# An attention and feed-forward kernel: the weight blocks of TensorE moved to 144 and 192 bytes past the moving rows

## The chip, the cores and the metric

One core of a Trainium2 chip runs the whole program. The metric is device time in microseconds (us), the median of three runs. TensorE (PE in the profile) multiplies, VectorE (DVE), ScalarE (ACT) and GpSimd (POOL) do the rest, and SyncE (SP) issues most of the DMAs.

## The reference

```
q, k, v: (4, 8, 768, 64)   x = attention output, reshaped to (3072, 512)
keep   = (key < n_sink) or (0 <= query - key < window)      n_sink 4, window 128
a      = softmax(where(keep, q k^T / 8, -1e9));  x = a v
h      = x @ w_in            (512 -> 2048)
out    = (h - tanh(h)) @ w_out   (2048 -> 512)
```

All values are float32.

## The kernel before

The 3072 tokens are cut into twelve chunks of 256 (`chunks`), the 2048 inner features into eight groups of 256 (`NG`). A step is one pair (chunk, group); there are 96 of them in the list `order`. The first three chunks (cc below 3) run early with weights that lie in SBUF; the other nine stream their first weights from DRAM through a ring of seven slots (`stream`, L784).

A float32 operand is split into a high and a low part of type float32r, and a product is the sum of high by high, high by low and low by high. So a step needs in `mm1` (L794 to 807) 2 x 4 x 3 = 24 products of 128x128 weights with 256 moving columns of x, and 24 x 96 = 2304 in all. The second half of a step comes in two kinds. In 41 steps it is `mm2` (L869 to 877): 12 products with 512 moving columns each, 492 in all. In the other 55 it is `mm7` (L907 to 911), a scheme of seven half-size products: 21 products of 256 columns, 1155 in all. The scores of the later chunks (L524) are 288 products of 260 columns.

For TensorE a product is two instructions. The weight load brings the *stationary* block, 128 values (512 bytes) of each partition, into the array; the multiplication then passes the *moving* rows through it, 256 columns being 1024 bytes of each partition. In `mm1` the weights are stationary and x moves; in `mm2` and `mm7` the gated activations (`ghbuf`, `glbuf`) are stationary and the weights of the second matrix move.

Tiles come from pools, and a pool's place in SBUF follows from the order in which the pools are opened and from the sizes of the tiles. This sets the byte at which each operand starts on its partition. In the program before, modulo 256: the weight tiles of `wpool` start at 0; the ring in `rpool` at 64, since `wtile` (L317) leaves out `FAR` = 80 elements; its second half `spare`, `ghbuf` and `glbuf` at 64; the x parts of `xall` at 0 for the later chunks and at 64 for chunks 0 and 1 (`x_high`, L678 to 686); the x parts of chunk 2 at 64 (high, `bpool`) and 0 (low, `hpool`). Since the blocks follow each other in steps of 512 bytes, the distance from the moving rows to the stationary block, modulo 256, is the same for all products of a kind:

| products | moving at | stationary at | distance | count |
|---|---|---|---|---|
| L807, chunks 3 to 11 | 0 | 64 | 64 | 1728 |
| L911 | 0 | 64 | 64 | 1155 |
| L807, chunks 0 to 2 | 64 or 0 | 0 or 64 | 192 (448), 0 (120), 64 (8) | 576 |
| L877 (512 columns) | 0 | 64 | 64 | 492 |
| L524 (260 columns) | 0, 16, 128, 144 | 64 | 64, 48, 192, 176 | 288 |
| L666 (512 columns) | 0 | 192 | 192 | 24 |

The order of the instructions on each engine is found at build time by a planner (`Work.order`) from costs and due times that are numbers in the code. It knows nothing of addresses.

Of the kernel before, what the change touches and what calls it, by code (L numbers as in the profile page):

```python
# [18 lines left out]
P = 128  # L19
# [20 lines left out]
@with_exitstack  # L40
def kernel(
    ctx: ExitStack,
    tc: tile.TileContext,
    qd: bass.AP,
    kp: bass.AP,
    vp: bass.AP,
    vs: bass.AP,
    nsw: bass.AP,
    w_in: bass.AP,
    w_out: bass.AP,  # L50
    xd: bass.AP,
    out: bass.AP,
):
    nc = tc.nc

    cpool = ctx.enter_context(tc.tile_pool(name="cpool", bufs=1))
    ident = cpool.tile([P, P], F32, tag="ident", name="ident")
    nswi = cpool.tile([P, 32], I32, tag="nswi", name="nswi")[:, :4]

    pts = cpool.tile([P, NPAIR, 2, 4, P], F32, tag="pt", name="pt")  # L60
    early = []
    for m in range(2):
        first = pts[:, m].rearrange("p h a b -> p (h a b)")
        early.append((first[:, :KW], first[:, KW : KW + 2 * CH].rearrange("p (h s) -> p h s", h=2)))
    et = mybir.EngineType
    with tc.manual_schedule(engines={et.PE, et.SP, et.DVE, et.Activation, et.Pool}):

        scr = pts[:, 2, 0]
        nc.sync.dma_start(nswi, nsw.partition_broadcast(P))
        for m in range(2):  # L70
            k, q = early[m]
            nc.sync.dma_start(k, kp[0, m, :, :KW])
            _load_pair(nc, q, qd[0, 2 * m : 2 * m + 2, :, :CH], True)
            if m == 0:
                make_identity(nc, ident)
                nc.gpsimd.iota(scr[:, 0, :].bitcast(I32), pattern=[[-1, P]], base=0, channel_multiplier=1)
                nc.gpsimd.iota(scr[:, 1, :].bitcast(I32), pattern=[[1, P]], base=0, channel_multiplier=0)
        masks = _masks(nc, cpool, nswi, scr)
        _, (nlo, nhi, wlo, whi) = nc.values_load_multi_w_load_instructions(
            nsw[0:1, 0:4], skip_runtime_bounds_check_because="every value takes one of the two branches"  # L80
        )
        bad = nhi | whi | ((nlo + 3) >> 3) | ((wlo - 1) >> 7)


        WARM = 3
        with tc.tile_pool(name="warm", bufs=1, space=PSUM) as wp:
            warm = wp.tile([P, P], F32, tag="warm", name="warm")
            for _ in range(WARM):
                nc.tensor.matmul(warm, lhsT=ident, rhs=ident, start=True, stop=True)

    with tc.If(bad == 0) as cmp:
        _banded(tc, qd, kp, vp, vs, masks, w_in, w_out, ident, pts, early, out)
    with cmp.Else():
        _general(tc, qd, kp, vp, nswi, w_in, w_out, ident, xd, out)

# [8 lines left out]
        nc.sync.dma_start(q[r, h, :], src[h, r])  # L104


def _masks(nc, pool, nswi, scr):

    mask = pool.tile([P, 3, TS], F32, tag="mask", name="mask")
    above = pool.tile([P, P], F32, tag="above", name="above")
    below = pool.tile([P, P], F32, tag="below", name="below")
    after = pool.tile([P, P], F32, tag="after", name="after")
    lim = pool.tile([P, 2], F32, tag="lim", name="lim")
    diff, col, tmp = (scr[:, i, :] for i in range(3))
    nc.gpsimd.memset(mask[:, 0, :NSK], NEG)
    nc.vector.tensor_copy(diff, diff.bitcast(I32))
    nc.vector.tensor_copy(col, col.bitcast(I32))  # L120
    nc.vector.tensor_scalar(above, diff, 0.0, None, op0=ALU.is_lt)
    nc.vector.tensor_scalar(below, diff, 0.0, None, op0=ALU.is_le)
    nc.vector.tensor_scalar(after, diff, 0.0, None, op0=ALU.is_gt)
    nc.vector.scalar_tensor_tensor(diff, above, float(P), diff, op0=ALU.mult, op1=ALU.add)
    nc.vector.tensor_scalar(tmp, above, NEG, None, op0=ALU.mult)
    nc.vector.tensor_copy(lim[:, 0:1], nswi[:, 0:1])
    nc.vector.tensor_copy(lim[:, 1:2], nswi[:, 2:3])
    n_sink, window = lim[:, 0:1], lim[:, 1:2]
    nc.vector.tensor_scalar(mask[:, 2, NSK:], diff, window, NEG, op0=ALU.is_ge, op1=ALU.mult)
    nc.vector.tensor_scalar(col, col, n_sink, NEG, op0=ALU.is_ge, op1=ALU.mult)  # L130
    nc.vector.tensor_tensor(mask[:, 0, NSK:], mask[:, 2, NSK:], tmp, op=ALU.min)
    nc.vector.tensor_tensor(mask[:, 0, NSK:], mask[:, 0, NSK:], col, op=ALU.max)

    near, edge, sink = diff[:, :NSK], tmp[:, :NSK], col[:, :NSK]
    nc.vector.tensor_scalar(near, near, window, None, op0=ALU.is_lt)
    nc.vector.tensor_tensor(edge, edge, near, op=ALU.mult)
    nc.vector.tensor_tensor(mask[:, 1, :NSK], edge, sink, op=ALU.min)

    def rest():
        nc.scalar.copy(mask[:, 1, NSK:], mask[:, 2, NSK:])  # L140
        nc.scalar.copy(mask[:, 2, :NSK], sink)

    return mask, above, below, after, rest
# [86 lines left out]
        return sorted(start, key=lambda n: (start[n], n)), start  # L230


def _banded(tc, qd, kp, vp, vs, masks, w_in, w_out, ident, pts, early, out):
    nc = tc.nc
    et = mybir.EngineType
    with ExitStack() as ctx:

        def pool(name, bufs, **kw):
            return ctx.enter_context(tc.tile_pool(name=name, bufs=bufs, **kw))

        cpool, wpool, rpool, gpool = (pool(n, 1) for n in ("cpool", "wpool", "rpool", "gpool"))
        vpool = pool("vpool", 3)
        bpool, wmpool, qpool, kpool, hpool, xpool = (
            pool(n, 1) for n in ("bpool", "wmpool", "qpool", "kpool", "hpool", "xpool")
        )
        pp, sm = pool("pp", 2), pool("sm", 4)
        xall = xpool.tile([P, 4 * NPAIR * CH + 16], F32R, tag="xall", name="xall")
        ps, ps_h = pool("ps", 1, space=PSUM), pool("ps_h", 2, space=PSUM)
        dpool = pool("dpool", 1, space=bass.MemoryType.DRAM)

        banks = {n: ps.tile([P, 512], F32, tag=n, name=n) for n in ("s0", "s1", "o0", "o1", "t", "x")}
# [3 lines left out]
        wide = wmpool.tile([P, 2, 4, TS], F32, tag="wide", name="wide")  # L255
        flat = wide.rearrange("p a b c -> p (a b c)")
        gbuf = gpool.tile([P, 8, P], F32, tag="gbuf", name="gbuf")
        ghbuf = gpool.tile([P, 2, 7, P], F32R, tag="ghbuf", name="ghbuf")
        glbuf = gpool.tile([P, 8, P], F32R, tag="glbuf", name="glbuf")
        wscr = dpool.tile([NG, P, 2 * WG], F32, tag="wscr", name="wscr")  # L260
        bscr = dpool.tile([NG, P, 5, DM // 2], F32, tag="bscr", name="bscr")
        kscr = dpool.tile([2, P, 2, DM // 2], F32, tag="kscr", name="kscr")
# [33 lines left out]
        def home(cc):  # L296

            return cc if cc < 3 else cc % 2

        def raw(u):  # L300
            return u < RAW

# [9 lines left out]
        lent = {u: ((1, 7), (1, 5), (1, 6), (0, 6))[(u - 4) // 2] for u in range(4, RAW)}  # L312
        place_of = {}

        FAR = 80

        def wtile(k, g, dtype, name):  # L317
            if k == 0 and g % NSLOT == 1:
# [10 lines left out]
        def load_qk(u):  # L329
            cc, p, b, c = unit(u)  # L330

            def lend():
                if u == 3:
                    if u not in place_of:
                        place_of[u] = gpool.tile([P, 3 * WG // 2], F32, tag="spare", name="qk3")
                    return place_of[u]
                if lent[u] not in place_of:
                    k, g = lent[u]
                    place_of[lent[u]] = wpool.tile([P, 2 * WG], F32, tag=wtag(k, g), name=f"qk{u}")
                return place_of[lent[u]][:, u % 2 * WG : u % 2 * WG + WG]  # L340
# [72 lines left out]

        sides = cpool.tile([P, 4], F32, tag="sides", name="sides")
        sidei = cpool.tile([P, 16], I32, tag="sidei", name="sidei")[:, :4]
        half, odd = sides[:, 0:2], sides[:, 2:4]
        vsink = cpool.tile([P, 2, P], F32R, tag="vsink", name="vsink")
        vraw = cpool.tile([P, P], F32, tag="vraw", name="vraw")  # L420
# [53 lines left out]
        def split(u):  # L474
# [2 lines left out]

            def k_high(h):
                if h == 0:
                    t = hpool.tile([P, NPAIR * CH], F32R, tag="ha", name=f"ks{u}")  # L480
                    ks[u] = t[:, : 2 * (KW + 24)].rearrange("p (h k) -> p h k", h=2)[:, :, :KW]
                r = slice(64 * h, 64 * h + 64)
                nc.scalar.copy(ks[u][r, h, :], kt[u][r, :])  # L483
# [23 lines left out]
        def scores(u, t):  # L507
# [21 lines left out]
            def merge():  # L529
                ps = sps[u, t]  # L530
                if t == 0:
                    if slot(u) > 1:
                        pr[u] = wide[:, slot(u) - 2]
                    else:
                        pr[u] = pp.tile([P, 4, TS], F32, tag="p", name=f"p{u}")
                    st[u] = sm.tile([P, 12], F32, tag="st", name=f"st{u}")
                for h in range(2):
                    if kind > 0:
                        nc.vector.copy_predicated(ps[h][:, TS:WIN], above.bitcast(U32), ps[h][:, :P])
# [102 lines left out]
        def attend(cc, p0, pairs):  # L642
# [35 lines left out]
            def x_high(i):  # L678
                if p0 == 0 and i == 0:
                    if home(cc) == 2:  # L680
                        xh[cc] = bpool.tile([P, NPAIR, CH], F32R, tag="hb", name=f"xh{cc}")
                        xl[cc] = hpool.tile([P, NPAIR, CH], F32R, tag="ha", name=f"xl{cc}")
                    else:
                        at = 2 * NPAIR * CH * (1 - home(cc)) + 16 * (cc < 3)
                        both = xall[:, at : at + 2 * NPAIR * CH].rearrange("p (k n c) -> p k n c", k=2, n=NPAIR)
                        xh[cc], xl[cc] = both[:, 0], both[:, 1]
                r = slice(p0 + 2 * i, p0 + 2 * i + 2)
# [96 lines left out]
        def stream(n, j):  # L784
# [2 lines left out]
            if "a" not in ring:  # L787
                ring["a"] = wtile(0, 1, F32R, "ring").rearrange("p (i c) -> p i c", i=4)
            if i > 3 and "b" not in ring:
                ring["b"] = gpool.tile([P, 3, WG // 2], F32R, tag="spare", name="spare")  # L790
            ring[i] = ring["b"][:, i - 4, :] if i > 3 else ring["a"][:, i, :]
            nc.sync.dma_start(ring[i].bitcast(F32), wscr[g][:, j * WG // 2 : (j + 1) * WG // 2])

# [20 lines left out]

        def halves(n):
            r = n % 2
            return ghbuf[:, r].rearrange("p b t -> p (b t)")[:, : 2 * CH], glbuf.rearrange("p b t -> p (b t)")[:, r * 2 * CH : (r + 1) * 2 * CH]

        def gate(n):
            g0 = gbuf.rearrange("p b t -> p (b t)")[:, : 2 * CH]  # L820
# [542 lines left out]
```

## Time and profile before

| | us |
|---|---|
| median of three runs | 678.68 |
| the three runs | 681.78, 678.13, 678.68 |
| span of the profiled execution | 676.2 |

The profiled execution's span, from its first instruction to its last, is 676.2 us; what lies around it in a timed run is the remaining 2.5 us of the median. PE is TensorE's multiplication, PEld its weight load, which runs beside the multiplication before it. The chain view follows the work back from the last instruction, each time to what released it; a row such as "2.72 PE h L807 x24" is 24 products that start one behind the other in 2.72 us, so 113 ns apart. This distance from start to start is the price of a product here; the duration of one (about 280 ns) is the time through the pipeline.

### The profile page before, as it was taken

The numbers are of one execution on the slowest core, as the hardware profiler recorded it, in microseconds if no ns is written. First come the engines' busy times: TensorE is split into PE (matmuls) and PEld (weight loads), VectorE is DVE, ScalarE is ACT, GpSimd is POOL, SyncE is SP. The second block draws the span as 40 slices with busy tenths as digits, with TensorE's granted clock in tenths as the row PEclk, the third lists the DMA queues.
The fourth block names the chain that finished last, engine by engine and source line by source line (L and its number), as shares of the span: only waits on it lengthen the run. The fifth ranks groups of instructions, "written<-read, shape, count | busy, mean of one in ns | idle before, by whom it ended". The sixth has DMA issues, their size and how long they took to land.

```text
span 676.2 us, 14570 instructions
## 1 busy us (share of the span) xinstructions
PE 655.5 (97%) x5099; PEld 603.3 (89%) x5099; DVE 531.8 (79%) x1365; ACT 412.6 (61%) x1056; POOL 204.0 (30%) x363
## 2 busy tenths in 40 slices
PE   6899999999999999999999999999999999999995
PEld 4677899998988899889999999999999999999995
DVE  6889998964898975567798898888988878855654
ACT  4986443435998876556776667567667567632331
POOL 5454000001995443344523323332223322300100
PEclk9999999999999999999999999999999999999998
DMA  5878797786998677799977767867777766657861
GB/s 177 266 262 269 266 295 263 270 287 175 191 203 274 203 217 223 227 280 266 300 217 240 224 199 207 260 196 203 227 231 216 242 199 199 198 165 207 270 198 37
DMA packets 79341, 152.96 MB, mean 226 GB/s; under 512 B 9564, under 2 KB 25564, under 8 KB 79260
## 3 DMA queue, kind: packets, MB, share of 16 engines
q1 hardware_dynamic: 65884, 121.65, 57.4%
q0 software_dynamic: 13376, 30.30, 16.4%
q8 instruction: 42, 0.69, 0.4%
q14 instruction: 39, 0.32, 0.1%
HBM read 131.47 MB, written 20.45 MB: 225 GB/s over the span
## 4 chain that ended last, share of the span: by engine, by line
PE 73%; ACT 7%; DVE 5%; DMA 5%; POOL 4%; issue 4%; POOLq 0%; SPq 0%; DVEq 0%; ACTq 0%
PE h L807 30%; PE s L911 10%; PE o L911 7%; PE o L877 6%; PE x L672 3%; PE s L877 3%; DMA w<-bscr 2%; PE t L609 2%; PE t L672 2%; PE t L877 2%; PE t L524 2%; PE x L877 2%; ACT p L575 2%; PE x L524 1%; ACT p L549 1%
## 5 line engine op out<-in xcount | busy, mean ns | idle before, releaser
L807 PE MATMUL h<-xall,ring 128*128 128x256 f32 x990 | 130.9, 279 | 0.0
L807 PEld LDWEIGHTS h<-xall,ring 128*128 128x128 f32 x990 | 121.2, 188 | 0.9 <-PE t L672 0.2
L826 ACT ACTIVATE gbuf<-h 128x512 f32<-128x512 f32 x96 | 57.1, 595 | 84.6 <-PE h L807 55.2
L356 POOL DMA_DIRECT2D qraw<-qd x36 | 29.3, 813 | 222.4 <-DVE q L496 198.0
L807 PE MATMUL h<-xall,spare 128*128 128x256 f32 x738 | 96.2, 277 | 0.0
L807 PEld LDWEIGHTS h<-xall,spare 128*128 128x128 f32 x738 | 90.0, 188 | 0.5
L549 ACT ACTIVATE p<-p,st 128x132 f32<-128x132 f32 x168 | 66.9, 400 | 26.8 <-DVE st L541 25.5
L845 ACT CAST ghbuf<-gbuf 128x896 fp32r<-128x896 f32 x55 | 51.9, 943 | 49.3 <-DVE gbuf L842 48.8
L848 DVE TENSOR_TENSOR glbuf<-gbuf,ghbuf 128x896 fp32r<-128x896 f32 x55 | 60.3, 1096 | 19.7 <-ACT ghbuf L845 16.0
L575 ACT ACTIVATE p<-p,st 128x132 f32<-128x132 f32 x168 | 54.2, 394 | 3.9 <-DVE st L570 3.5
L829 DVE TENSOR_TENSOR gbuf<-h,gbuf 128x512 f32<-128x512 f32 x55 | 37.8, 687 | 19.1 <-ACT gbuf L826 18.7
L877 PE MATMUL o<-w,ghbuf 128*128 128x512 f32 x192 | 50.8, 399 | 0.3
L629 POOL TENSOR_TENSOR pt<-pt,after 128x512 f32<-128x512 f32 x32 | 44.4, 1386 | 22.0 <-ACT pt L626 21.3
L807 PE MATMUL h<-xall,w 128*128 128x256 f32 x384 | 50.5, 282 | 0.0
L807 PEld LDWEIGHTS h<-xall,w 128*128 128x128 f32 x384 | 48.5, 188 | 1.6
L829 DVE TENSOR_TENSOR h<-h,gbuf 128x512 f32<-128x512 f32 x41 | 28.5, 694 | 19.1 <-ACT gbuf L826 19.0
L488 DVE TENSOR_TENSOR ks<-kraw,ks 64x392 fp32r<-64x392 f32 x72 | 40.4, 562 | 3.4 <-ACT ks L483 1.1
L877 PEld LDWEIGHTS o<-w,ghbuf 128*128 128x128 f32 x192 | 33.8, 188 | 6.8 <-ACT ghbuf L832 0.9
L623 DVE TENSOR_TENSOR pt<-t,below 128x512 f32<-128x512 f32 (+1 forms) x48 | 28.8, 600 | 12.6 <-PE t L609 7.4
L483 ACT CAST ks<-kraw 64x392 fp32r<-64x392 f32 x72 | 37.1, 515 | 2.2 <-DMA kraw<-kp 1.4
L911 PE MATMUL s<-edge,ghbuf 128*128 128x256 f32 x220 | 35.5, 280 | 0.1
L835 DVE TENSOR_TENSOR glbuf<-h,ghbuf 128x512 fp32r<-128x512 f32 x41 | 28.1, 685 | 9.1 <-ACT ghbuf L832 9.1
(174 smaller groups left out, 1560.8 us busy)
## 6 DMA issues: line engine op xcount, KB each, us to landing
ring<-wscr SPq DMA_DIRECT2D x165, 256.0 KB, 4.3
spare<-wscr SPq DMA_DIRECT2D x123, 256.0 KB, 4.6
qraw<-qd POOLq DMA_DIRECT2D x36, 256.0 KB, 5.0
wraw<-w_in SPq DMA_DIRECT2D x16, 512.0 KB, 6.0
wraw<-w_out SPq DMA_DIRECT2D x16, 512.0 KB, 5.7
wscr<-w SPq DMA_DIRECT2D x16, 512.0 KB, 6.0
kraw<-kp POOLq DMA_DIRECT2D x36, 196.0 KB, 4.6
v<-vp POOLq DMA_DIRECT2D x18, 256.0 KB, 3.4
```

Source lines behind the costliest of these rows:

```text
L483: nc.scalar.copy(ks[u][r, h, :], kt[u][r, :])
L488: (nc.gpsimd if KP else nc.vector).tensor_tensor(k[o, h, :], t[r, :], k[r, h, :].bitcast(F32), op=ALU.subtract)
L549: nc.scalar.activation(e, e, AF.Exp, bias=st[u][:, j : j + 1], scale=-1.0, accum_out=st[u][:, 4 + j : 5 + j],)
L575: nc.scalar.activation(pr[u][:, j, :], pr[u][:, j, :], AF.Copy, scale=s[:, 8 + j : 9 + j])
L629: nc.gpsimd.tensor_tensor(w[:, :, 0, :], w[:, :, 0, :], after.unsqueeze(1).to_broadcast([P, 4, P]), op=ALU.mult)
L807: nc.tensor.matmul(hps[n][:, f, :], lhsT=w, rhs=x, start=r == 0, stop=r == 11)
L826: nc.scalar.activation(g0, h(), AF.Tanh)
L829: nc.vector.tensor_tensor(g0 if strassen(n) else h(), h(), g0, op=ALU.subtract)
L845: nc.scalar.copy(ghbuf[:, n % 2], gbuf[:, 1:, :])
L848: nc.vector.tensor_tensor(glbuf[:, :7, :], gbuf[:, 1:, :], ghbuf[:, n % 2].bitcast(F32), op=ALU.subtract)
L877: nc.tensor.matmul(sums_of(n, cc, t), lhsT=a[:, f, t * P : (t + 1) * P], rhs=wt[1, g][:, (0, 1, 0)[i], f, :], start=first and not low and ...
L911: nc.tensor.matmul(acc, lhsT=a[:, b, :], rhs=factor(g, m, part % 2), start=g == 0 and part == 0 and m in (4, 1, 2, 7), stop=closes(n) and ...
```

## The change

Only places in SBUF change: pools are opened in another order, small tiles are put together in one (`small`, `stats`), and some tiles get a few unused elements ahead of them. The instructions, their order on every engine and what each waits for are the same as before; so are all shapes. The core of the diff:

```diff
-        vpool = pool("vpool", 3)
-        bpool, wmpool, qpool, kpool, hpool, xpool = (
-            pool(n, 1) for n in ("bpool", "wmpool", "qpool", "kpool", "hpool", "xpool")
+        kpool, qpool, pp, spool, vpool = pool("kpool", 1), pool("qpool", 1), pool("pp", 2), pool("spool", 1), pool("vpool", 3)
+        wmpool, hpool, ghpool, bpool, xpool, sm = (
+            pool(n, 1) for n in ("wmpool", "hpool", "ghpool", "bpool", "xpool", "sm")
         )
-        pp, sm = pool("pp", 2), pool("sm", 4)
-        xall = xpool.tile([P, 4 * NPAIR * CH + 16], F32R, tag="xall", name="xall")
+        SHIFT, XOFF, HOFF = 12, 24, 20
+        xall = xpool.tile([P, 4 * NPAIR * CH + XOFF + 28], F32R, tag="xall", name="xall")
...
+        glflat = cpool.tile([P, 4 + SHIFT + 8 * P], F32R, tag="glbuf", name="glbuf")[:, 4:]
...
-        ghbuf = gpool.tile([P, 2, 7, P], F32R, tag="ghbuf", name="ghbuf")
-        glbuf = gpool.tile([P, 8, P], F32R, tag="glbuf", name="glbuf")
+        ghbuf = ghpool.tile([P, 4 + 14 * P], F32R, tag="ghbuf", name="ghbuf")[:, 4:]
...
-        FAR = 80
+        FAR = 36
...
-                        at = 2 * NPAIR * CH * (1 - home(cc)) + 16 * (cc < 3)
+                        at = 2 * NPAIR * CH * (1 - home(cc)) + xoff(cc)
...
-            return ghbuf[:, r].rearrange("p b t -> p (b t)")[:, : 2 * CH], glbuf.rearrange("p b t -> p (b t)")[:, r * 2 * CH : (r + 1) * 2 * CH]
+            a, b = shift(n), shift(n) + r * 2 * CH
+            return ghbuf[:, r].rearrange("p b t -> p (b t)")[:, a : a + 2 * CH], glflat[:, b : b + 2 * CH]
```

`xoff(cc)` is 24 elements, and 28 more for cc below 3; `shift(n)` is always 12 elements (48 bytes). In the changed program the weight tiles start at 192 modulo 256, the ring, `spare`, `ghbuf` and `glbuf` at 80, the halves that `mm2` reads at 128, and x at 192 (later chunks), 48 (chunks 0 and 1, and the low part of chunk 2) or 96 (the high part of chunk 2). The distances become:

| products | moving at | stationary at | distance | count |
|---|---|---|---|---|
| L807 of before, chunks 3 to 11 | 192 | 80 | 144 | 1728 |
| L911 of before | 192 | 80 | 144 | 1155 |
| L807 of before, chunks 0 to 2 | 48 or 96 | 192 or 80 | 144 (392), 96 (112), 32 (56), 240 (16) | 576 |
| L877 of before (512 columns) | 192 | 128 | 192 | 492 |
| L524 of before (260 columns) | 48, 64, 176, 192 | 96 | 48, 32, 176, 160 | 288 |

## Rows read from the trace of the kernel before

**Rows 1.** The page: busy time of each engine, and TensorE's clock in 40 slices.
```profile
PE 655.5 (97%) x5099; PEld 603.3 (89%) x5099; DVE 531.8 (79%) x1365; ACT 412.6 (61%) x1056; POOL 204.0 (30%) x363
PEclk9999999999999999999999999999999999999998
```
**Rows 2.** Windows: us of the stretch; busy us and instructions of each engine; clock; DMA.
```profile
120.00:160.00 40.00, 39.32 (x252) 35.37 (x251) 27.55 (x34) 15.91 (x27) 1.34 (x2) 1.00 0.74 260
...
300.00:350.00 50.00, 49.81 (x390) 45.70 (x390) 36.70 (x93) 32.66 (x81) 20.73 (x33) 1.00 0.95 274
...
600.00:650.00 50.00, 50.00 (x441) 49.84 (x440) 30.05 (x54) 15.78 (x21) 2.75 (x4) 1.00 0.75 223
```
**Rows 3.** Waits of PE: who waited for whom; us in total, times, longest.
```profile
PE s L517 <- DMA qk<-qd: 3.3, 2, 1.7
PE warm L89 <- POOL pt L103: 3.2, 1, 3.2
PE t L609 <- ACT pt L616: 1.9, 3, 1.0
```
**Rows 4.** The page: the chain that ended last, by engine.
```profile
PE 73%; ACT 7%; DVE 5%; DMA 5%; POOL 4%; issue 4%; POOLq 0%; SPq 0%; DVEq 0%; ACTq 0%
```
**Rows 5.** The chain from 600 us on, in order of time: start, us, what.
```profile
614.86 2.72 PE h L807 x24
...
629.48 0.68 PE o L911 x6
```
**Rows 6.** The chain from 75 to 112 us: chunks 1 and 2.
```profile
84.79 2.80 PE s L877 x12
87.59 2.86 PE h L807 x24
...
93.25 2.83 PE h L807 x24
```
**Rows 7.** The chain from 585 to 600 us: transposes and the sink products.
```profile
586.33 0.44 PE t L609 x4
...
590.06 0.23 PE x L666
590.30 0.23 PE t L666
```
**Rows 8.** The chain from 196 to 226 us.
```profile
204.70 0.48 PE s L524 x4
...
212.15 6.33 DMA kraw<-kp
...
221.87 1.86 PE o L877 x8
```
**Rows 9.** The chain from 300 to 350 us.
```profile
311.00 8.30 DMA w<-bscr
...
327.44 0.52 issue
328.00 1.73 POOL pt L629
329.73 1.14 POOL w L1009
```

## What was predicted

> **What bounds the kernel now.** I read the page first, then the windows by stage, then the waits of PE, and last the chain in order of time. The page is to show which engine is full: PE is busy for 655.5 of 676.2 us and its clock stands at full speed in all slices but the last [rows 1]. The windows show whether that fullness is real: in the stretch from 600 to 650 us PE is busy for 50.00 us with 441 products, so they follow each other at 113.4 ns, and even in the crowded stretch from 300 to 350 us it is busy for 49.81 [rows 2]. The waits confirm it: the longest entry of the list is 3.3 us in total, and it belongs to the start of the program [rows 3]. So the kernel is as long as its products are numerous and dear. No engine needs to be faster; a product has to start sooner after the one before it. The chain is TensorE for 73% of the span [rows 4]. The rest of the chain lies in a few places where a release came just in time, and it matters below for what a faster PE can keep.
>
> The price of a product is then read from the chain, as the time of a run of equal products by their number. Late products of 256 columns, at distance 64: 2.72 us for 24 and 0.68 us for 6, both 113.3 ns [rows 5]. Early ones: 2.83 us for 24, or 117.9 ns, in a step of chunk 1, all at distance 192; 2.86 us for 24, or 119.2 ns, in a step of chunk 2, where 16 are at 192 and 8 at 0 [rows 6]. Same shape, same engine, full clock [rows 1], no idle time ahead of them; the distance is the difference that I know of. Products of 512 columns at distance 64: 2.80 us for 12, or 233.3 ns [rows 6], and 1.86 us for 8, or 232.5 [rows 8].
>
> **What no row shows** is a product of 256 columns at distance 144. I bound it. The cheapest product of the full width of the array in these rows is the transpose (128 columns in full float32): four take 0.44 us, 110 ns each, whatever the distance [rows 7]. The nearest row for a disturbed one is 119.2 ns [rows 6]. So a product at 144 should cost between 110 and 119.2 ns against 113.3 now: from 3.3 ns less to 5.9 ns more. I take 111, and this is the choice on which the forecast hangs. A straight line between 64 (113.3) and 192 (117.9) would give 116 at 144. But a distance is one on a circle of 256: the dearest rows have distance 0 among them, 64 and 192 both lie 64 bytes from 0, and 144 lies 112 bytes from it, farther than either. If what costs is the nearness of the two addresses, 144 should be cheaper than both, and the nearest row is then the 110. I keep 1 ns above it.
>
> **The parts.**
> First, the late products: 1728 of L807 and 1155 of L911 go from 64 to 144. 2883 x (113.3 - 111) = 6.6 us less. Ends: 2883 x 3.3 = 9.5 less, 2883 x 5.9 = 17.0 more.
> Second, the early products. 392 of the 576 come to 144, from 118 to 119: 392 x (118.3 - 111) = 2.9 us less; ends 3.3 less (at 110) and 0.4 more (at 119.2). The other 184 come to 96, 32 and 240, which no row shows either; I leave them at their price, with ends 184 x 8 = 1.5 less and as much more. These steps stand on the chain without a break [rows 6], so what they save is kept.
> Third, 492 products of 512 columns go from 64 to 192. The sink products L666 have 512 columns at 192 now: 0.23 us each, two of them 0.24 apart [rows 7]. To the two digits of the row that is 225 to 240 ns, the same as 233. I take 230: 492 x 3.3 = 1.6 us less. Ends: twice 110, so 492 x 13 = 6.4 less, and 240, so 3.3 more.
> Fourth, 288 products of 260 columns at 120 ns [rows 8] go from 64, 48, 192 and 176 to 48, 32, 176 and 160. Two of the four distances stay in the set, so nothing, with ends of 288 x 5 = 1.4 us on both sides.
> Fifth, the tiles that are put together or moved for VectorE, ScalarE and GpSimd. Each of their instructions is the same, in the same place and with the same waits. At nothing: they run beside PE, which almost never waits for them [rows 3].
> Gross: 6.6 + 2.9 + 1.6 = 11.1 us.
>
> **What is late next.** A PE that runs 2% ahead meets the places where it is released just in time. The chain leaves PE for a key load of 6.33 us at 212 [rows 8], and around 300 to 350 us for a weight transfer of 8.30 us and the GpSimd work that issues the adding DMAs [rows 9], while the DMA engines are 95% busy [rows 2]. By rows 4 PE has 73% of the chain and is busy for 97% of the span; if gains in the missing quarter were all lost, 75% would remain. Those chains contain waits for earlier products too, which come sooner as well. I keep 87%: 11.1 x 0.87 = 9.7 us. The profiled execution then spans 676.2 - 9.7 = 666.5, and with the 2.5 us around it the time is 669.0, against the median of 678.68.
>
> **A rule against the change.** The rows say that products of one shape cost 113.3 ns in one stage and 118 to 119 in another [rows 5, 6]. The Trainium skill (TensorE: Matmul & The Clock Gate, Step-by-step: what each phase is for) says that TensorE has two independent read ports into SBUF, one for the moving rows and one for weight loads, so that loading the next block takes no bandwidth from the running product. By that the distance of two addresses can't matter, and the change gives nothing; the second rival is that case. The same page (Back-to-back issue gap) puts a product of 256 columns at N/2.4 + 2.5, so 109.2 ns as an estimate, which no product of 256 columns reaches in these rows. By it as the price at 144 the first term would be 2883 x 4.1 = 11.8 us.
>
> **Rivals.**
> 1. 144 is a worse distance than 64 (slower). Mechanism: at 144 each late product pays what the early ones at 192 pay now, 117.9 ns. For it: of the distances with a row, 64 is the cheapest, the block now starts at 80 modulo 256 and no longer at a multiple of 64, and the 260-column products, at 48 to 192, stand at 120 ns [rows 8], above 113.3 x 260/256 = 115.1. Against it: no row has 144 itself. Price: 2883 x 4.6 = 13.3 us more, all of it kept since a slower PE is the bound everywhere, less 1.6 for the 512 columns: 678.7 + 11.7 = 690. It decides as soon as a late product takes over 113.9 ns, where 2883 x 0.6 eats the 1.6 us of the wide ones. Halfway, every second product disturbed, 684.
> 2. No change. Either the dearer early products are a matter of their stage and not of addresses, or 113.3 ns is already the least for 256 columns. For it: no 256-column run of these rows is under 113 ns. Against the first reading: the window from 120 to 160 us, with the dear products, has less work on VectorE, ScalarE and GpSimd per us than 300 to 350 [rows 2], and chunks 1 and 2 differ within one stage [rows 6]. Time: 678.7 where addresses do nothing, 676 where only the early and wide products gain.
> 3. All late products fall to 110, and the wide ones to their end: 9.5 + 3.3 + 6.4 = 19.2, times 0.87, 16.7 less: 662.
> 4. The change does not do quite what its words say: 184 products of 256 columns are not at 144. It is priced in the second part at 1.5 us either way and moves no case.
>
> **How the numbers follow.** No change from what a measurement can tell is 0.5%, 3.4 us on both sides. The forecast with its neighbours (665 to 675.3): 0.42. Rival 3 (655 to 665): 0.20. Rival 2 (675.3 to 682.1): 0.17. Rival 1, whole or in part (above 682.1): 0.21. So faster 0.62, same 0.17, slower 0.21. The likeliest case's own range is 665 to 675. The range that should hold 8 in 10 has to reach over the no-change case and half of rival 1, and down to the ends of the prices: 657 to 686.
>
> **What would show it.** In the profile after: 24 late products of L807's counterpart in 2.64 to 2.68 us instead of 2.72 for the forecast, 2.83 or more for rival 1, 2.72 for rival 2; the number of products in 600 to 650 us up from 441 to about 450, or down to 425; a step of chunk 1 at the same price as a late one; twelve wide products under 2.80 us. The waits of PE should grow a little around 212 and 300 to 350 us. I am wrong if late products take longer than 113.3 ns, or if they take less and the span does not follow, which would put the bound in those stretches.

## The result, and the profile after

The changed kernel takes 687.63 us (median of four runs, 686.98 to 689.1), against 679.13 us for the kernel before in the same comparison; the ratio is 1.0121, with a 95% interval of 1.009 to 1.0153. The change makes the kernel slower, by 8.5 us between the medians. The profiled execution spans 685.3 us, 9.1 more than before.

The page of the changed kernel, busy time and the chain by engine:

```profile
PE 666.9 (97%) x5099; PEld 618.4 (90%) x5099; DVE 531.6 (78%) x1365; ACT 413.1 (60%) x1056; POOL 203.2 (30%) x363
...
PE 83%; POOL 4%; DVE 4%; ACT 3%; DMA 2%; issue 2%; SPq 0%; POOLq 0%; DVEq 0%; ACTq 0%
```

VectorE, ScalarE and GpSimd work as long as before, to 0.8 us [rows 1]. TensorE alone works 11.4 us longer, and its share of the chain grows from 73% to 83% [rows 4]. The windows of the changed kernel:

```profile
120.00:160.00 40.00, 39.26 (x254) 35.52 (x253) 27.96 (x33) 15.92 (x27) 1.35 (x2) 1.00 0.75 261
300.00:350.00 50.00, 50.00 (x390) 46.71 (x389) 36.64 (x93) 32.04 (x78) 20.25 (x31) 1.00 0.94 276
600.00:650.00 50.00, 50.00 (x419) 50.00 (x419) 29.36 (x54) 14.93 (x20) 2.75 (x4) 1.00 0.68 206
```

From 600 to 650 us there are 419 products instead of 441 [rows 2], at full clock and without a gap: 119.3 ns each instead of 113.4. Early, 254 instead of 252. (From 300 to 350 us both kernels have 390, but that stretch mixes products of many shapes.) So the loss is a dearer product, and only a late one. The chain of the changed kernel, late and early (L819, L924 and L890 are L807, L911 and L877 of before):

```profile
605.50 2.88 PE h L819 x24
635.38 0.72 PE s L924 x6
...
653.99 2.84 PE h L819 x24
...
84.93 2.75 PE s L890 x12
87.68 2.85 PE h L819 x24
93.30 2.78 PE h L819 x24
```

Up to 643 us late products at distance 144 stand at 2.88 / 24 = 120.0 ns, in both halves of a step, where they stood at 113.3 [rows 5]; the last steps stand at 2.84 / 24 = 118.3. The wide ones went from 233.3 to 229.2 ns, a step of chunk 2 from 119.2 to 118.8 and one of chunk 1 from 117.9 to 115.8 [rows 6]. This last pair is the clue: chunk 1 has distance 144 too, but its stationary blocks start at 192 modulo 256, and those of the late products at 80.

The sum: over the whole trace the mean time from the start of a late product to the next start, pauses of over 150 ns left out, was 114.2 ns before and is 119.0 after. 2883 x 4.8 = 13.8 us more. Read in the same way, the wide ones give back 492 x 3.0 = 1.5 and chunks 0 and 1 384 x 1.8 = 0.7. That is 11.6 us, near the 11.4 that PE is busy longer. Its idle time fell by 2.3 us (from 676.2 - 655.5 = 20.7 to 685.3 - 666.9 = 18.4), which leaves the 9.1.

### The profile page after: what moved, and what is told of

Its sections match the earlier page's. It is cut to its first block, busy times and chain, and to the rows that moved or that the text cites. A ratio compares the mean times of both kernels' runs of the same rounds, so it can differ in the third digit from the quotient of the medians.

```text
span 685.3 us, 14570 instructions
## 1 busy us (share of the span) xinstructions
PE 666.9 (97%) x5099; PEld 618.4 (90%) x5099; DVE 531.6 (78%) x1365; ACT 413.1 (60%) x1056; POOL 203.2 (30%) x363
## 4 chain that ended last, share of the span: by engine, by line
PE 83%; POOL 4%; DVE 4%; ACT 3%; DMA 2%; issue 2%; SPq 0%; POOLq 0%; DVEq 0%; ACTq 0%
PE h L819 35%; PE s L924 11%; PE o L924 8%; PE o L890 7%; PE x L682 3%; PE s L890 3%; PE t L619 3%; PE t L682 2%; PE t L534 2%; PE t L890 2%; PE x L534 2%; PE x L890 2%; POOL edge L1022 1%; PE s L534 1%; DMA v<-vp 1%
## 5 line engine op out<-in xcount | busy, mean ns | idle before, releaser
L819 PE MATMUL h<-xall,ring 128*128 128x256 f32 x990 | 135.3, 284 | 0.0
L819 PEld LDWEIGHTS h<-xall,ring 128*128 128x128 f32 x990 | 125.1, 189 | 0.7 <-PE t L682 0.2
L819 PE MATMUL h<-xall,spare 128*128 128x256 f32 x738 | 99.9, 283 | 0.0
L819 PEld LDWEIGHTS h<-xall,spare 128*128 128x128 f32 x738 | 93.2, 189 | 0.5
L559 ACT ACTIVATE p<-p,st 128x132 f32<-128x132 f32 x132 | 52.6, 400 | 21.4 <-DVE st L551 20.3
L890 PE MATMUL o<-w,ghbuf 128*128 128x512 f32 x192 | 50.4, 397 | 0.2
L819 PE MATMUL h<-xall,w 128*128 128x256 f32 x384 | 49.9, 280 | 0.0
L819 PEld LDWEIGHTS h<-xall,w 128*128 128x128 f32 x384 | 47.9, 188 | 1.5
L585 ACT ACTIVATE p<-p,st 128x132 f32<-128x132 f32 x132 | 42.6, 394 | 2.6 <-DVE st L580 2.4
L890 PEld LDWEIGHTS o<-w,ghbuf 128*128 128x128 f32 x192 | 33.8, 188 | 6.3 <-ACT ghbuf L845 0.8
L924 PE MATMUL o<-w,ghbuf 128*128 128x256 f32 x220 | 36.4, 284 | 0.0
L924 PE MATMUL s<-edge,ghbuf 128*128 128x256 f32 x220 | 36.3, 284 | 0.0
```

The costliest lines, as they stand in the source:

```text
L559: nc.scalar.activation(e, e, AF.Exp, bias=st[u][:, j : j + 1], scale=-1.0, accum_out=st[u][:, 4 + j : 5 + j],)
L585: nc.scalar.activation(pr[u][:, j, :], pr[u][:, j, :], AF.Copy, scale=s[:, 8 + j : 9 + j])
L819: nc.tensor.matmul(hps[n][:, f, :], lhsT=w, rhs=x, start=r == 0, stop=r == 11)
L890: nc.tensor.matmul(sums_of(n, cc, t), lhsT=a[:, f, t * P : (t + 1) * P], rhs=wt[1, g][:, (0, 1, 0)[i], f, :], start=first and not low and ...
L924: nc.tensor.matmul(acc, lhsT=a[:, b, :], rhs=factor(g, m, part % 2), start=g == 0 and part == 0 and m in (4, 1, 2, 7), stop=closes(n) and ...
```

## The experiments

**A sweep of 256 columns (m256).** The program loads six tiles, and then only multiplies; `d` is the distance, `al` the place of the stationary block. The edit is shortened.

```diff
+    for al in (64, 80, 96, 192):
+        for d in range(0, 256, 16):
+            mov = place(al - d); st = place(al)          # both modulo 256
+            for rep in range(2):
+                for k in range(24):                      # blocks in the order of mm1
+                    nc.tensor.matmul(o, lhsT=buf[:, st_k : st_k + 128], rhs=buf[:, mov_k : mov_k + 256], ...)
```

> Only a sweep, no attention and no feed-forward: 64 streams of 48 products of 128x128 by 256 columns, in the order of the kernel's own first half-step (each first stationary block twice, each second once), at 16 distances (0 to 240 in steps of 16 bytes) times 4 places of the stationary block (64, 80, 96 and 192 modulo 256). Nothing else runs beside them. Theory A, the distance modulo 256 alone sets the price: at each distance the four places agree, 64 stands at 113 ns, 144 at 119, 192 at 118, 0 at 118 to 120. Theory B, what costs is that the stationary block begins off a multiple of 64: the streams at 64 and 192 are cheap at distance 144 (113 or less), those at 80 and 96 stand at 119 at nearly every distance, 64 included. Theory C, the traffic of other engines or the moved small tiles: all 64 streams stand at one price.

Each distance has a line of its own: L106 is 0, and every second line from there 16 bytes more, so L114 is 64, L124 is 144 and L130 is 192. The chain is the sweep in order; the first rows have the stationary block at 64, those from 108 us on at 80, from 199 us at 96 and from 290 us at 192:

```profile
18.08 5.74 PE b L106 x48
...
40.85 5.46 PE b L114 x48
46.31 5.72 PE b L116 x48
...
57.66 5.60 PE b L120 x48
63.26 5.76 PE b L122 x48
69.02 5.50 PE b L124 x48
...
131.39 5.45 PE b L114 x48
...
159.70 5.76 PE b L124 x48
...
250.43 5.50 PE b L124 x48
...
340.99 5.50 PE b L124 x48
```

Nothing runs here but TensorE, and still the price goes from 5.45 to 5.76 us per 48, 113.5 to 120 ns, with the distance. Theory C is out. Distance 64 is at its cheapest in both places. Distance 144 is nearly as cheap (5.50; the first eleven products of the stream stand at 116 to 121 ns, the rest at 113.3 from start to start) with the block at 64, and as dear as any (5.76, 120 ns) with the block at 80. It was the same at 96 and 192 as at 64. So neither A nor B as put is right: 144 is a good distance if the stationary block starts in the right place, and 64 is good everywhere. No stream of the 64 goes below 113.3.

**The same for 512 columns (m512).**

> The same sweep with 512 columns, the stationary block at 64 and at 128 modulo 256, 32 streams of 48 products. Theory A: distance 64 at 233 ns, distance 192 at 229 to 230, at both places. Theory B: the places 64 and 128 are both multiples of 64, so distances that are multiples of 64 agree and the others are dearer. Theory C: all streams at one price.

The chain at distance 0, 64 and 192, with the block at 64:

```profile
22.81 10.89 PE b L106 x48
...
67.36 11.20 PE b L114 x48
...
156.75 10.99 PE b L130 x48
```

Measured, in the second half of each stream: 233.3 ns at distance 64, 228.9 at 192, 226.7 at 0, all others between 231.1 and 234.6; the two places agree within 0.3. Theory A holds for the wide products at these two places, which are both multiples of 32; others were not tried. And 192 was not the best choice: 0 is, and it costs two products of 256 columns at 113.3, to 0.1 ns.

**The change with its 256-column distance undone (d64).** The order of the pools (but for one) and the packed tiles are kept.

```diff
-        SHIFT, XOFF, HOFF = 12, 24, 20
+        SHIFT, XOFF, HOFF = 32, 48, 0
-        glflat = cpool.tile([P, 4 + SHIFT + 8 * P], ...)[:, 4:]
+        glflat = cpool.tile([P, SHIFT + 8 * P], ...)
-        ghbuf = ghpool.tile([P, 4 + 14 * P], ...)[:, 4:]
+        ghbuf = ghpool.tile([P, 32 + 14 * P], ...)[:, 32:]
-            return XOFF + (28 if cc < 3 else 0)
+            return 32 if cc < 3 else XOFF
-        FAR = 36
+        FAR = 16
```

(and `spare` 16 instead of 12 elements into its tile, `bpool` opened ahead of `ghpool`, the high part of the keys 16 elements into its tile).

> The changed kernel with its order of pools and its packed small tiles kept, but all late products of 256 columns at distance 64 again (moving at 0, stationary at 64), 504 of the 576 early ones at 64 too (moving at 192, stationary at 0) and 72 at 128, and the 512-column products at 192 as in the change. Theory A and B alike: late products back at 113.3 to 114.2 ns, early ones at 114 instead of 118, 512 columns at 229.7; against the kernel before 504 x 4 ns + 492 x 3.4 ns = 3.7 us less, so about 675. If only the distance of the early and wide ones fails to help, 679. Theory C, the packing or the moved tiles of the other engines cost the time: it stays at 686 to 688.

678.72 us, ratio to before 1.0001 (0.9978 to 1.0024). Undoing the distance takes back the whole loss: theory C is out in the full kernel too, and the rest of the change has no cost that this comparison, good to some 1.6 us, can show. But the 3.7 us did not come. Two places of its chain show why:

```profile
601.66 2.72 PE h L819 x24
...
642.88 2.83 PE h L819 x24
```

The same 24 products, at the same distance, from the same places, cost 113.3 ns in one step and 117.9 in another. The start times show where it changes: at about 635 us two products in the middle of a stream start 126 and 193 ns after the one before, and from there on all late products, of both halves of a step, stand at 117.8. Over the whole trace the late products come to 114.8 ns on the mean instead of 114.2 (1.9 us more), the early ones to 115.6 instead of 118.3 and the wide ones to 230.4 instead of 233.1 (2.8 us less). So the rows themselves promise 0.9 us, not 3.7.

**Distance 144 with the block 16 bytes lower (x144), and distance 64 with the block at 80 (x64).** Both start from the changed kernel and aim at the 1728 late products of the first half-step. x64 touches nothing else; in x144 72 early products, which read the ring too, go from distance 32 to 16 or from 240 to 224.

```diff
# x144
-            return rpool.tile(...)[:, FAR:]
+            return rpool.tile(...)[:, FAR - 4 : FAR - 4 + 2 * WG]      # spare likewise, 8 for 12
-            return XOFF + (28 if cc < 3 else 0)
+            return XOFF + (28 if cc < 3 else -4)
# x64
-            return XOFF + (28 if cc < 3 else 0)
+            return XOFF + (28 if cc < 3 else 20)
```

> The changed kernel, in which the ring, its second half and the x parts of the later chunks lie 16 bytes lower: the 1728 late products of the first half-step stay at distance 144, but their stationary blocks begin at 64 modulo 256 instead of 80. Everything else is as in the change. Theory B2 (from the sweep: 144 is as cheap as 64 where the stationary block begins at a multiple of 32, and dear at 80): these products fall from 119 to 113 or 114 ns, 1728 x 5 = 8.6 us less than the change, 679. Theory A (the distance alone sets the price): nothing moves, 687.6.

> The changed kernel, in which only the x parts of the later chunks move by 80 bytes: the 1728 late products of the first half-step have distance 64, their stationary blocks still begin at 80. Theory B2 with the sweep (64 is cheap at every place, 80 included): 113 to 114 ns, 679, as in the other run. Theory B1 (a stationary block off a multiple of 32 is dear by itself, at any distance): 119 ns, 687.6.

x64: 681.58 us, ratio 1.0038 (1.0024 to 1.0053), 6 us less than the change. x144: 685.76 us, ratio 1.0105 (1.0081 to 1.013), 1.9 less, which four runs of each hardly tell from the change; the prices in the trace do. Their chains, x144 first:

```profile
602.37 2.77 PE h L819 x24
607.65 2.77 PE h L819 x24
```
```profile
602.63 2.74 PE h L819 x24
607.85 2.74 PE h L819 x24
```

x64 does nearly what was expected: 114.2 ns here (114.9 on the mean over the whole trace), with the block still at 80, so B1 is out. x144 was expected at the same 679 and missed. The block's place does count (115.4 ns here, 120.0 in the change; 116.4 and 119.0 on the mean over the whole trace), but the stream does not start at the sweep's 113.3. The timeline of the first of these streams, with start and duration, happens to be cut in its middle by a change of tile:

```profile
602.21 1.57 PE L819 MATMUL h<-xall,spare 128*128 128x256 f32 x12
603.62 1.52 PE L819 MATMUL h<-xall,ring 128*128 128x256 f32 x12
604.98 0.40 PE L924 MATMUL s<-edge,ghbuf 128*128 128x256 f32 x2
```

From start to start the first twelve products take 1.41 us, 117.5 ns each, and the other twelve 1.36, 113.3 ns each. By the single start times it is the same in all 30 late steps with 24 or more products in a row: the first eleven stand at 118 on the mean, those behind them at 113.4. The sweep had these eleven dear products at distance 144 too, but in a stream of 48 they are easily overlooked; in one of 24 they are nearly half.

**The place of the block in all 16 steps (mal).**

```diff
-    for al in (64, 80, 96, 192):
-        for d in range(0, 256, 16):
+    for al in range(0, 256, 16):
+        for d in (64, 144, 0, 112):
```

> Only a sweep of 256 columns again: the stationary block at all 16 places modulo 256, at the distances 64, 144, 0 and 112. Theory B2: at distance 144 the eight places that are multiples of 32 stand at 113.3 ns and the eight others at 120; distance 64 stands at 113.3 at all places. If the rule is about multiples of 64, places 32, 96, 160 and 224 are dear at 144 as well (96 was cheap in the first sweep, so I don't expect it). If it is the moving rows that have to begin off a multiple of 32, the same split appears, since at 144 the two go together.

L115 is distance 64, L125 is 144; the block at 0, then at 16, 32 and 48:

```profile
18.79 5.46 PE b L115 x48
24.24 5.51 PE b L125 x48
...
41.20 5.45 PE b L115 x48
46.65 5.68 PE b L125 x48
...
63.76 5.45 PE b L115 x48
69.22 5.51 PE b L125 x48
...
86.18 5.45 PE b L115 x48
91.62 5.68 PE b L125 x48
```

At distance 144 the eight places that are multiples of 32 stand at 5.51 us, the other eight at 5.68; at 64 all sixteen at 5.45 to 5.46. Whether it is the stationary block or the moving rows that must lie so can't be told at 144, where the one at a multiple of 32 means the other is not. Nor is such a place good by itself: distance 0 takes 5.75 us at the multiples of 32 and 5.68 elsewhere. A block at 80 settled here at 118.3 ns and in m256 at 120.0, with other streams ahead of it: the same products again at two prices.

**A stream entered from wide products (mpair).**

```diff
+    for d in (64, 144):
+        for w in range(0, 256, 16):
+            for rep in range(2):
+                12 products of 512 columns at distance w        # L99, L101, ... by w
+                24 products of 256 columns at distance d        # L168, L170, ... by w; block at 64
```

> Only a sweep: 12 products of 512 columns at one of 16 distances, then 24 products of 256 columns at distance 64 or 144, the stationary blocks of the latter always at 64 modulo 256 (so a multiple of 32), each pair of streams twice. Theory H (a stream keeps the pace with which it is entered): the same 24 products stand at 113.3 ns after some distances of the wide ones and at 117 to 120 after others; after 0 at distance 64 they stand at 118, after 192 and 64 at 113.3; at distance 144 more of the 16 entries end in the slow pace than at 64. Theory N (the price belongs to the products alone, and the slow streams of the full kernels come from other engines' work): all 24-product streams stand at 113.3 whatever went before, at 64 and at 144.

The chain for d = 64: entered from w = 0, twice; from w = 16, twice; from w = 192. The last two rows are d = 144, entered from w = 32 and w = 64:

```profile
21.78 2.72 PE b L99 x12
24.50 2.83 PE b L168 x24
27.33 2.75 PE b L99 x12
30.08 2.83 PE b L168 x24
...
35.70 2.73 PE b L170 x24
...
41.22 2.83 PE b L170 x24
...
155.34 2.75 PE b L123 x12
158.09 2.73 PE b L192 x24
...
224.59 2.80 PE b L204 x24
...
246.81 2.72 PE b L208 x24
```

Theory N falls: TensorE works alone here, and the same products have different prices. Theory H holds at distance 64. There the 24 products take 2.73 or 2.83 us, and nothing in between is common. By the start times, 15 of the 32 streams stand at 117.8 ns from the first product to the last, and the other 17 come down to 113.3 within three products and stay there. What ran just before does not decide it alone: for 11 of the 16 distances of the wide products both entries end in the same pace, for five, w = 16 among them, each way once.

At distance 144, with the good place of the block, theory H does not hold, and the slow paces that it expected there don't last: all 32 streams reach 113.3 ns. Ten stand there from the first product, two after three dearer ones, and the other 20 after 6 to 13 products of 114 to 123 ns, which makes 114.7 to 116.4 over the stream. This run-in is what x144 has, and what leaves the step of chunk 1 in the changed kernel at 115.8: ten dear products, then 113.3.

**The cheapest rows put together (best).**

```diff
-        SHIFT, XOFF, HOFF = 32, 48, 0
+        SHIFT, XOFF, HOFF = 48, 48, 0
-        zr = cpool.tile([P, 16 + 2 * CH], F32R, ...)[:, 16:]
+        zr = cpool.tile([P, 2 * CH], F32R, ...)
```

(against d64: the wide products go from distance 192 to 0)

> A version that takes the cheapest row of both sweeps: 256 columns at distance 64 (late ones, and 504 of the early ones), 512 columns at distance 0, which the sweep puts at 226.7 ns against 233.3 at 64 and 228.9 at 192. If the sweep carries over: 492 x 6.5 = 3.2 us and 504 x 2.7 = 1.4 us less than the kernel before, less some 1 us lost where the chain leaves TensorE: 675.5. If what the wide products save is lost in waits for other engines: 678 to 679, as with the distances 64 and 192.

677.75 us, ratio to before 0.9972 (0.9958 to 0.9986): by the ratio 1.9 us faster than the kernel before, by the medians 10 faster than the change. Its chain has what mpair shows for w = 0 at distance 64:

```profile
84.47 2.74 PE s L890 x12
87.21 2.83 PE h L819 x24
...
602.34 2.72 PE h L819 x24
```

The wide products are cheaper, at 228 ns, and the early steps that follow them stand at 117.9 ns, although they have distance 64 now. In d64, where the wide ones are at 192, the early ones came to 115.6 on the mean; here to 117.5. Of the 31 streams at distance 64 that start right behind wide products, early and late, 30 stand at 117.7 to 118.2 ns here, and only 4 in d64 at 117.5 or more; the order of the work is the same, so it is the wide products' places that set the pace. So the gain of the wide products came (492 x 4.5 = 2.2 us against the kernel before), that of the early ones did not, and the late ones came to 114.6 instead of 114.2, 1.2 us more. What is left is 1.9 us of the 3.5 expected.

## Why the prediction was wrong

What bounds the kernel was right: the time followed the price of a product, and the engines whose tiles moved show no difference above 0.8 us.

The step that failed is the choice of 111 ns for a product at distance 144. It measured 120.0 ns in the undisturbed stretch and 119.0 on the mean. The working held two mistakes. The lower bound, 110, came from the transpose [rows 7], which is another kind of product; the sweep has no stream of 256 columns below 113.3, so distance 64 was at the bottom already, and the first term could hardly be a gain at any distance (at most 2883 x 0.9 = 2.6 us, from the mean of 114.2). Rival 2 had this as its second reading and I gave it too little. And the picture of a circle, where 144 is far from 0 and so cheap, is not what the sweep shows: 112 stands at 116.7, 128 at 119.9, 80 at 119.2 with the block at 64. Good distances are single places, not a slope. With 113.3 in its place the first term is 0; with the 119.0 and the 114.2 that the kernel has, it is the 13.8 us more.

Second part: the early products at 144 were to fall to 111; the step of chunk 1 came to 115.8. The sign was right, the size was a third. Third part: 230 ns was forecast for the wide products, 229.2 came: right. Fourth and fifth: no visible cost, right (the products of 260 columns stand at 120.2 ns on the mean after 120.3). The share kept by the critical chain did not matter for a loss, and no run tested it: in d64 the rows promise only 0.9 us, which its time can't show.

Rival 1 is what happened: 690 was its time, 687.6 was measured, and it was given a fifth. Its price, 117.9, was near the 119.0, but in part by luck: it was taken from distance 192, and 144 has such a price only where the block lies off a multiple of 32. Of what spoke for it the block's start off a multiple of 64 pointed the right way: mal puts the line at multiples of 32.

The Trainium skill (TensorE: Matmul & The Clock Gate, Step-by-step: what each phase is for) says that weight loads have a read port of their own and take nothing from the running product. In m256 TensorE works alone and the price moves by 6 to 7 ns with the addresses of the two operands, so for this data type the measurement decides against what the prediction drew from that rule, that addresses can't matter. The page's N/2.4 + 2.5 for a product by itself, 109.2 ns as an estimate for 256 columns (Back-to-back issue gap), is not reached either: 113.3.

What stays open: why some pairs of addresses cost more than others was not measured, nor what decides between the two paces at distance 64. Nor was the whole change tried with all its blocks on multiples of 32: tiles begin on multiples of 32 here, and at 144 the weight tiles, which move in L924, would all need padding.

## What to carry to other kernels

Where TensorE is full, the distance between the stationary block and the moving rows is a parameter worth up to 6% of a 256-column product; sweep it alone on the chip, with absolute places and not the difference only, before moving anything in the kernel. A price from such a sweep carries over only if the stream is entered as in the sweep and is as long, so read it product by product and measure the products together with those that run before them. And a cheaper price has to be bounded by a row of the same kind of product: where many runs in the trace end at the same least value, take that for the floor until a row shows less.

## What the runs showed of the hardware

- The least price of the two widths is proportional to their columns: 113.3 ns for 256 (m256), 226.7 for 512 (m512). At the full clock of 2.4 GHz that is 272 and 544 cycles, 17 for 16 columns.
- Distance 64 gives that price at every one of 16 places of the block (mal); distance 144 only at multiples of 32 (113.3 against 118.3 to 120.0), and often only after a run-in of up to 13 dearer products (mpair, x144).
- A stream of equal products at distance 64 has more than one lasting pace (113.3 or 117.8 ns). What ran before it has a part in the choice: of the 31 such streams that start right behind wide products, 30 stand at 117.7 to 118.2 ns in best (wide ones at distance 0) and 4 in d64 (at 192) at 117.5 or more.
